# Running batch 1's whole first FFT stage ahead of the FFN, with wide loads and early weights

## The chip, the core and the metric

One core of a Trainium2 chip. The metric is device time in microseconds (us) of one execution. Each profile is that of one of the timed runs; its span is some 2 us shorter than the run's time, because the time also holds what lies outside the first and last instruction. Some names recur: `dZ`, `dU` are the DRAM copies of two intermediates, `zt`, `ut` the SBUF tiles that they are read back into, and a *slot* is one step of the FFN loop: one group of matmuls with W_in (`psH`, then ReLU and square) and one with W_out (`psO`), 1.74 us of TensorE at full clock.

## The reference, cut

```python
def _attn_ref(x, filt_r, filt_i):                 # x: (8, 3008, 256)
    X = np.fft.rfft(x, axis=1)
    Y = X * (filt_r + 1j * filt_i)[None, :, :]    # one global filter, 1505 x 256
    return np.fft.irfft(Y, n=x.shape[1], axis=1).astype(np.float32)

def _moe_ref(x, w_in, w_out):                     # x: (24064, 256); W: 256 x 2048, 2048 x 256
    h = np.maximum(x @ w_in, 0.0)
    return (h * h @ w_out).astype(np.float32)
```

The second follows on the first: an FFT along the sequence, a product with the filter F, the inverse FFT, then an FFN with a squared ReLU.

## The kernel before

The FFT is done by matmuls in stages. Stage A (`psA`, result u) is followed by a change of layout, stage B (`psB`), the product with F on VectorE (`prod`), stage P (`psP`, result ze), a trip through DRAM (`dZ`, `zt`) and stage Y (`psY`, result yt). yt feeds the FFN. Batch 0 runs first, with nothing beside it; from then on each next batch's stages are put between the FFN's matmuls, slot by slot. Batch 0 has its own stage A: x is the stationary operand, and ScalarE and VectorE evict each PSUM bank into a transposed copy, uT.

```python
def chunk_a0(c):                               # batch 0, c = 0..3
    for k in range(2):
        for dt in range(2):
            ...                                # 8 matmuls of 96 columns into ps
            m = 32 * c + 16 * k
            o = uT[:, dt, :, m:m + 16].rearrange("p c (m q) -> p m c q", q=4)
            pv = ps[:, 0:384].rearrange("p (m c q) -> p m c q", m=4, q=4)
            if dt == 0: nc.scalar.copy(out=o, in_=pv)
            else:       nc.vector.tensor_copy(out=o, in_=pv)
```

uT is `[128, 2, 24, 128]` in float16, so for a fixed c the index m, q runs over neighbours and c steps by 128 elements, 256 bytes. PSUM is read in order, and each run of four q is 8 bytes side by side in SBUF.

What surrounds the FFN's start, in program order (`...` marks cuts):

```python
for r in range(14):                            # batch 0: stages B and P
    ...
    if r in (5, 8):
        load_x(1, r // 8); cast_x(1, r // 8, nc.gpsimd)    # 96-row tiles
    if r == 10: read_z(0, 0, (0,))
read_z(0, 1, (0,))
for c in range(2): read_z(0, c, (1,))
for c in range(2): chunk_a(1, c)               # half of batch 1's stage A
load_wout(); load_x(1, 2); load_x(1, 3)
for c in range(2, 4): read_z(0, c)
for c in range(2): write_u(1, c)
keep_warm(10)
for n in range(4): unit_y(0, n)                # then the FFN starts
...
for p in range(12):                            # batch 1's products, in slots 16 to 33
    r = t0 + (17 if b == 1 else 19) * p // 11
    put(r, 0, unit_b, b, p); put(r, 0, unit_s, b, p); put(r + 2, 1, unit_p, b, p)
```

Pools that matter: two x32 buffers, three u buffers, three ze buffers. A ze or u buffer is free again only when the DMA that wrote it to DRAM has landed (experiments 5 and 8 show such waits: 6.35 us for a u buffer, 5.26 us for a ze buffer).

## Time and profile before

| | us |
|---|---|
| median of the first three runs | 823.59 (821.54 to 827.16) |
| profiled run, its span | 826.93, 824.8 |
| ScalarE's table load (ACT_TABLE_LOAD): starts, takes | 12.02, 1.28 |
| last eviction of batch 0's stage A starts | 24.6 |
| first dZ write issued | 41.58 |
| output group of slot 8, slot 34, slot 40 starts | 75.84, 142.37, 156.69 |

The views that the prediction rests on stand in it. The first is the tile view of uT in the kernel before: line, engine, operation, count, then least, median and greatest ns of one instruction, the times of the first and last start, and the shapes.

```profile
L377 ACT CAST uT<-psA x8: 478/478/479, 14.0 to 24.2; 128x384 f16<-128x384 f32 x8
L379 DVE CAST uT<-psA x8: 557/557/558, 15.5 to 24.6; 128x384 f16<-128x384 f32 x8
```

```profile
20.00:40.00 20.00, 17.19 (x213) 14.94 (x211) 13.47 (x15) 12.14 (x17) 4.85 (x5) 0.97 0.52 192
```

The reader is to see that an eviction of 384 elements takes about half a microsecond (0.48 us on ScalarE, 0.56 on VectorE), and that TensorE is at almost full clock here (0.97).

### The profile page before, as it was taken

To read this page: it belongs to the slowest core of one execution; us is meant where nothing else is said; L and a number is where in the kernel's file an instruction comes from. 1 tells how busy PE (TensorE), PEld (TensorE's weight loads), DVE (VectorE), ACT (ScalarE), POOL (GpSimd) and SP (SyncE) were. 2 spreads that over 40 slices of the span, in tenths; PEclk is the share of its full clock that TensorE was granted. 3 is DMA by queue.
4 is the path that set the end of the run, shared out by engine and by line. 5 is a ranking of instruction groups with operands and counts; after the bars stand their busy time and mean duration, and the time that the engine had idled before them with its cause. 6 is when DMAs were issued, how large, how long until landed. Compare 5 with 4: busy or idle time off the path is not lost.

```text
span 824.8 us, 14748 instructions
## 1 busy us (share of the span) xinstructions
PE 787.3 (95%) x6080; PEld 553.7 (67%) x6080; DVE 547.7 (66%) x874; ACT 553.4 (67%) x708; POOL 32.6 (4%) x45
## 2 busy tenths in 40 slices
PE   5878987999999999999999999999999999999998
PEld 3744654666767667776668666786767767676666
DVE  4656566557975599656995579755995569654432
ACT  1655764676777777677777767776777767766664
POOL 4210132000000000000000000000000000000000
PEclk7998999999999999999999999999999999999999
DMA  9488454533681554624563346715555242431111
GB/s 367 174 243 205 141 141 118 126 93 126 165 205 41 142 163 128 170 63 156 141 174 83 105 144 166 187 37 169 133 145 143 64 153 77 108 73 39 39 39 52
DMA packets 87930, 107.94 MB, mean 131 GB/s; under 512 B 6208, under 2 KB 78656, under 8 KB 83392
## 3 DMA queue, kind: packets, MB, share of 16 engines
q1 hardware_dynamic: 87512, 106.59, 46.0%
q8 instruction: 47, 0.77, 0.4%
q10 hardware_dynamic: 288, 0.43, 0.2%
q14 instruction: 19, 0.16, 0.1%
q0 software_dynamic: 64, 0.00, 0.0%
HBM read 58.76 MB, written 48.23 MB: 130 GB/s over the span
## 4 chain that ended last, share of the span: by engine, by line
PE 83%; DMA 8%; DVE 6%; POOL 2%; ACT 1%; issue 1%; SPq 0%; POOLq 0%; DVEq 0%; ACTq 0%
PE psO L530 36%; PE psH L515 34%; PE psA L327 3%; PE psY L485 2%; DMA ut<-dU 2%; PE psB L408 2%; DVE prod L411 2%; PE psP L444 2%; DMA wout<-in_moe_w_out_dram 1%; DVE h L523 1%; DMA x<-in_x_dram 1%; DMA dZ<-ze 1%; DMA zt<-dZ 1%; POOL yf L420 1%; POOL yf L419 1%
## 5 line engine op out<-in xcount | busy, mean ns | idle before, releaser
L519 ACT ACTIVATE h<-psH 128x1024 f16<-128x1024 f32 x376 | 384.9, 1024 | 199.9 <-PE psH L515 197.5
L530 PE MATMUL psO<-sWout,h 128*128 128x256 f16 x3008 | 390.7, 273 | 3.3 <-DVE h L523 3.3
L515 PE MATMUL psH<-yt,sWin 128*128 128x512 f16 (+7 forms) x1728 | 389.0, 353 | 3.1 <-DVE yt L494 2.5
L530 PEld LDWEIGHTS <-h 128*128 128x128 f16 x3008 | 291.3, 98 | 83.6 <-DVE h L523 3.9
L523 DVE TENSOR_TENSOR h<-h 128x1024 f16<-128x1024 f16 x376 | 254.0, 685 | 101.3 <-ACT h L519 99.9
L515 PEld LDWEIGHTS <-sWin 128*128 128x128 f16 x1728 | 159.9, 98 | 104.1 <-issue 6.2
L411 DVE TENSOR_TENSOR prod<-psB,sF 128x1024 f16<-128x1024 f32 x96 | 116.7, 1220 | 9.7 <-PE psB L408 6.5
L494 DVE CAST yt<-psY 128x376 f16<-128x376 f32 x64 | 35.1, 549 | 62.2 <-PE psY L485 62.2
L446 ACT CAST ze<-psP 128x512 f16<-128x512 f32 x96 | 55.9, 585 | 28.6 <-PE psP L444 25.1
L334 DVE CAST u<-psA 96x512 f16<-96x512 f32 x52 | 35.7, 687 | 49.5 <-PE psA L327 49.5
L537 ACT COPY ost<-psO 128x512 f32<-128x512 f32 x94 | 55.5, 590 | 7.5 <-PE psO L530 5.8
L426 DVE TENSOR_TENSOR yf<-prod,yf 128x512 f16<-128x512 f16 x84 | 35.7, 425 | 19.4 <-POOL yf L420 16.9
L485 PEld LDWEIGHTS <-zt 112*128 112x128 f16 x512 | 34.8, 98 | 15.8 <-issue 6.2
L485 PE MATMUL psY<-sC,zt 112*128 112x94 f16 x512 | 42.1, 205 | 2.8 <-DMA zt<-dZ 1.4
L327 PE MATMUL psA<-x,sC 94*96 94x512 f16 x104 | 40.1, 386 | 0.9 <-DVE x L313 0.9
L408 PE MATMUL psB<-ut,sSB 128*128 128x256 f16 x192 | 36.6, 272 | 3.3 <-DVE prod L411 2.3
L444 PE MATMUL psP<-yf,sSP 128*128 128x256 f16 x168 | 32.1, 273 | 4.1 <-DVE prod L411 3.0
L408 PEld LDWEIGHTS <-sSB 128*128 128x128 f16 x192 | 18.6, 98 | 24.7 <-issue 6.0
L492 ACT CAST yt<-psY 128x376 f16<-128x376 f32 x64 | 29.8, 467 | 4.1 <-PE psY L485 4.0
L313 DVE CAST x<-x 94x2048 f16<-94x2048 f32 x26 | 31.6, 1216 | 0.0
L332 ACT CAST u<-psA 96x512 f16<-96x512 f32 x52 | 29.8, 572 | 0.4 <-PE psA L327 0.4
L419 DVE COPY yf<-prod 64x512 f16<-64x512 f16 x72 | 20.9, 290 | 2.5
(53 smaller groups left out, 229.7 us busy)
## 6 DMA issues: line engine op xcount, KB each, us to landing
x<-in_x_dram SPq DMA_DIRECT2D x24, 768.0 KB
dZ<-ze SPq DMA_DIRECT2D x32, 384.0 KB
zt<-dZ SPq DMA_DIRECT2D x64, 192.0 KB
dU<-u SPq DMA_DIRECT2D x28, 384.0 KB
out_dram<-ost SPq DMA_DIRECT2D x32, 256.0 KB
out_dram<-ost SPq DMA_DIRECT2D x64, 128.0 KB
ut<-dU SPq DMA_DIRECT2D x7, 1024.0 KB
ut<-dU SPq DMA_DIRECT2D x7, 512.0 KB
```

The source lines that it names most:

```text
L327: nc.tensor.matmul(ps[0:96, :], sSA, x16s[(b, c)][:, 2 * i:2 * i + 2, :], start=True, stop=True)
L334: nc.vector.tensor_copy(out=o, in_=pv)
L408: nc.tensor.matmul(ps[:, i * D:(i + 1) * D], sSB[:, 2 * p + i, :], uts[b][:, 2 * p + i, :], start=True, stop=True)
L411: nc.vector.tensor_mul(out=prod, in0=ps.rearrange("p (a d) -> p a d", d=D).unsqueeze(1).to_broadcast([128, 2, 2, D]), in1=sF[:, :, 2 * p:2 ...
L444: nc.tensor.matmul(ps[:, i * D:(i + 1) * D], sSP[:, c2, :], prod[:, i, :], start=True, stop=True)
L446: nc.scalar.copy(out=zes[(b, c)][:, 2 * i6:2 * i6 + 2, :], in_=ps.rearrange("p (a d) -> p a d", d=D))
L485: nc.tensor.matmul(ps[:, 94 * jj:94 * jj + 94], zt[:, 4 * (g % 2) + jj, dt * 128:(dt + 1) * 128], sSY, start=True, stop=True)
L515: nc.tensor.matmul(ps[:, i, o:o + n], sWin[:, dt, jt * 128:(jt + 1) * 128], yts[b][:, dt, r:r + n], start=(dt == 0), stop=(dt == 1))
L519: nc.scalar.activation(out=h2[:, 2 * s:2 * s + 2, :], in_=ps, func=AF.Relu)
L523: nc.vector.tensor_mul(out=v, in0=v, in1=v)
L530: nc.tensor.matmul(pso[g][:, t % 2, :], h2s[g][:, jt, t * 128:(t + 1) * 128], sWout[:, jt, :], start=(jt == 0), stop=(jt == NJT - 1))
L537: nc.scalar.copy(out=ost, in_=pso[g])
```

## The change

The intent: have everything that batch 1 and the FFN need ready before the FFN starts, so that the slots hold fewer waits. Batch 1's stage A runs whole ahead of the FFN, on the same wide tiles (128 rows) that batch 0 uses; to share the weights `s0`, their columns are put in the order (q, c). W_in loads early into the x buffers, W_out in two halves, the first ahead of the last dZ write. The u read moves from slot 12 to 4, and batch 1's twelve products spread over slots 8 to 33. F is cast behind stage A, and a tiny ScalarE copy pulls its table load to the start (it starts at 1.61 us in the changed kernel, at 12.02 before).

```diff
-    S0 = S0.reshape(128, 6, 2, 2, NC).transpose(0, 1, 4, 2, 3)
...
+    nc.scalar.copy(out=zero[0:1, 0:1], in_=zero[0:1, 1:2])     # table load early
     keep_warm(14)
... in chunk_a, batch 1
-                nc.tensor.matmul(banks[i][0:96], sSA, x16s[(b, c)][:, m, :], start=True, stop=True)
+                nc.tensor.matmul(o, s0[:, c // 2, :], xw16[(b, 2 * (c % 2))][:, m, :],
+                                 start=True, stop=False)
+                nc.tensor.matmul(o, s0[0:120, 2 + c, :], xw16[(b, 1)][0:120, m, :],
+                                 start=False, stop=True)
... in chunk_a0, batch 0
-                o = uT[:, dt, :, m:m + 16].rearrange("p c (m q) -> p m c q", q=4)
-                pv = ps[:, 0:384].rearrange("p (m c q) -> p m c q", m=4, q=4)
+                o = uT[:, dt, :, m:m + 16].rearrange("p c (m q) -> p m q c", q=4)
+                pv = ps[:, 0:384].rearrange("p (m q c) -> p m q c", m=4, q=4)
... in the plan of slots, b == 1
-        put(12 if b == 1 else 14, 1, read_u, b)
-        t0 = 16 if b == 1 else 18
+        put(4 if b == 1 else 14, 1, read_u, b)
+        t0 = 8 if b == 1 else 18
-            r = t0 + (17 if b == 1 else 19) * p // 11
+            r = t0 + (25 if b == 1 else 19) * p // 11
... ahead of the FFN
-        if r in (5, 8):
-            load_x(1, r // 8)
-            cast_x(1, r // 8, nc.gpsimd)
+        for k in {5: (0,), 8: (1, 2)}.get(r, ()):
+            load_wide(1, k)
+            cast_wide(1, k, nc.gpsimd)
         if r == 10:
             read_z(0, 0, (0,))
+            load_wout(0)
+    for k in range(2):
+        cast_wout(k, nc.gpsimd)
     read_z(0, 1, (0,))
+    chunk_a(1, 0)
+    chunk_a(1, 2)
     for c in range(2):
         read_z(0, c, (1,))
-    ...                                                        # as printed above
+    write_u(1, 0); chunk_a(1, 1); write_u(1, 2); load_wout(1)
+    for n in range(2): unit_y(0, n)
+    chunk_a(1, 3)
+    for n in range(2, 4): unit_y(0, n)
+    write_u(1, 1); write_u(1, 3)
```

With the new column order, the eviction of batch 0 reads PSUM in order again, but the innermost index is now c: it writes single elements, 256 bytes apart.

More of the change, by code (lines that the diff above doesn't have):

```diff
@@ L210, with load_wide, cast_wide @@
     nc.scalar.dma_start(out=sPF, in_=dPF.ap().rearrange("p (w q) -> p w q", q=128))
-    x0 = []
-    v0 = xrows[0:2048, :].rearrange("(p m) d -> p m d", m=16)
-    v1 = xrows[2048:3072, :].rearrange("(p m) d -> p m d", m=8)
-    for k, v in enumerate((v0[:, 0:8, :], v1, v0[:, 8:16, :])):
-        t = (p_h2 if k == 2 else p_x32).tile([128, 8, D], F32, tag="h2" if k == 2 else "x32",
-                                             name=f"x0_{k}")
-        nc.sync.dma_start(out=t, in_=v)
-        x0.append(t)
+    xw32, xw16 = {}, {}
+    def load_wide(b, k):
+        v0 = xrows[b * S:b * S + 2048, :].rearrange("(p m) d -> p m d", m=16)
+        v1 = xrows[b * S + 2048:b * S + 3072, :].rearrange("(p m) d -> p m d", m=8)
+        pool = p_h2 if (b, k) == (0, 2) else p_x32
+        t = pool.tile([128, 8, D], F32, tag="h2" if pool is p_h2 else "x32", name=f"xw_{b}_{k}")
+        nc.sync.dma_start(out=t, in_=(v0[:, 0:8, :], v1, v0[:, 8:16, :])[k])
+        xw32[(b, k)] = t
+    def cast_wide(b, k, eng):
+        t = p_x16.tile([128, 8, D], F16, tag="x16", name=f"xw16_{b}_{k}")
+        for i in range(2):
+            m = slice(4 * i, 4 * i + 4)
+            eng.tensor_copy(out=t[:, m, :], in_=xw32[(b, k)][:, m, :])
+        xw16[(b, k)] = t
+    for k in range(3):
+        load_wide(0, k)
     f32s = []
@@ L289, with load_win, cast_win, load_wout @@
     w32s = {}
-    def load_win():
-        w32s[0] = p_h2.tile([128, 2, DFF], F32, tag="h2", name="win32")
-        nc.sync.dma_start(out=w32s[0], in_=moe_w_in.rearrange("(t r) j -> r t j", r=128))
-    def load_wout():
-        w32s[1] = p_h2.tile([128, NJT, 256], F32, tag="h2", name="wout32")
-        nc.sync.dma_start(out=w32s[1], in_=moe_w_out.rearrange("(jt r) c -> r jt c", r=128))
-    def cast_win():
-        for k in range(4):
-            nc.gpsimd.tensor_copy(out=sWin[:, :, 512 * k:512 * k + 512],
-                                  in_=w32s[0][:, :, 512 * k:512 * k + 512])
-    def cast_wout(k):
-        nc.vector.tensor_copy(out=sWout[:, 4 * k:4 * k + 4, :],
-                              in_=w32s[1][:, 4 * k:4 * k + 4, :])
+    def load_win(k):
+        w32s[k] = p_x32.tile([128, DFF], F32, tag="x32", name=f"win32_{k}")
+        nc.sync.dma_start(out=w32s[k], in_=moe_w_in[128 * k:128 * k + 128, :])
+    def cast_win(k):
+        for j in range(2):
+            c = slice(1024 * j, 1024 * j + 1024)
+            nc.gpsimd.tensor_copy(out=sWin[:, k, c], in_=w32s[k][:, c])
+    def load_wout(k):
+        if k == 0:
+            w32s[2] = p_h2.tile([128, NJT, 256], F32, tag="h2", name="wout32")
+        c = slice(8 * k, 8 * k + 8)
+        nc.sync.dma_start(out=w32s[2][:, c, :],
+                          in_=moe_w_out.rearrange("(jt r) c -> r jt c", r=128)[:, c, :])
+    def cast_wout(k, eng=nc.vector):
+        c = slice(4 * k, 4 * k + 4)
+        eng.tensor_copy(out=sWout[:, c, :], in_=w32s[2][:, c, :])
     x16s, us, uts, prods, zes, zts, yts = {}, {}, {}, {}, {}, {}, {}
@@ L345, in chunk_a @@
                 m = slice(4 * k + 2 * i, 4 * k + 2 * i + 2)
-                nc.tensor.matmul(banks[i][0:96], sSA, x16s[(b, c)][:, m, :],
-                                 start=True, stop=True)
+                o = banks[i][0:96]
+                nc.tensor.matmul(o, s0[:, c // 2, :], xw16[(b, 2 * (c % 2))][:, m, :],
+                                 start=True, stop=False)
+                nc.tensor.matmul(o, s0[0:120, 2 + c, :], xw16[(b, 1)][0:120, m, :],
+                                 start=False, stop=True)
             eng = pair_engine()
@@ L368, in chunk_a0 @@
                     d = slice(128 * dt, 128 * dt + 128)
-                    nc.tensor.matmul(o, x016[2 * (c % 2)][:, m, d], s0[:, c // 2, :],
+                    nc.tensor.matmul(o, xw16[(0, 2 * (c % 2))][:, m, d], s0[:, c // 2, :],
                                      start=True, stop=False)
-                    nc.tensor.matmul(o, x016[1][0:120, m, d], s0[0:120, 2 + c, :],
+                    nc.tensor.matmul(o, xw16[(0, 1)][0:120, m, d], s0[0:120, 2 + c, :],
                                      start=False, stop=True)
                 m = 32 * c + 16 * k
-                o = uT[:, dt, :, m:m + 16].rearrange("p c (m q) -> p m c q", q=4)
-                pv = ps[:, 0:384].rearrange("p (m c q) -> p m c q", m=4, q=4)
+                o = uT[:, dt, :, m:m + 16].rearrange("p c (m q) -> p m q c", q=4)
+                pv = ps[:, 0:384].rearrange("p (m q c) -> p m q c", m=4, q=4)
                 if dt == 0:
@@ L567, in fft_plan @@
                     unit_y, 0, n)
-            for k in range(4):
-                put(3 + k, 1, cast_wout, k)
-            for c in range(2, 4):
-                put(3 + 2 * c, 0, cast_x, 1, c)
-        t0 = 4 if b == 1 else 6
-        for a in range(8 if b == 1 else 0, 16):
+            for k in range(2, 4):
+                put(2 + k, 1, cast_wout, k)
+        t0 = 6
+        for a in range(0 if b > 1 else 16, 16):
             put(t0 + a // 2, a % 2, unit_a, b, a)
-        put(12 if b == 1 else 14, 1, read_u, b)
-        t0 = 16 if b == 1 else 18
+        put(4 if b == 1 else 14, 1, read_u, b)
+        t0 = 8 if b == 1 else 18
         for p in range(12):
-            r = t0 + (17 if b == 1 else 19) * p // 11
+            r = t0 + (25 if b == 1 else 19) * p // 11
             put(r, 0, unit_b, b, p)
@@ L602, in run @@
             f(*a)
-    x016 = [p_x16.tile([128, 8, D], F16, tag="x16", name=f"x016_{k}") for k in range(3)]
     uT = p_h2.tile([128, 2, NC, 128], F16, tag="h2", name="uT")
     for k, eng in enumerate((nc.vector, nc.vector, nc.gpsimd)):
-        for i in range(2):
-            m = slice(4 * i, 4 * i + 4)
-            eng.tensor_copy(out=x016[k][:, m, :], in_=x0[k][:, m, :])
-    f16s.append(p_h2.tile([128, 2, QF + D], F16, tag="h2", name="f16"))
-    for im in range(2):
-        nc.gpsimd.tensor_copy(out=f16s[0][:, im, QF:], in_=nyq[:, im, :])
-        for e in (slice(0, 1504), slice(1504, QF)):
-            nc.gpsimd.tensor_copy(out=f16s[0][:, im, e], in_=f32s[im][:, e])
+        cast_wide(0, k, eng)
     def load_const(t, d, k):
@@ L626 @@
         load_const(sSPx[k], dSPx, k)
+    for k in range(2):
+        load_win(k)
     for c in (0, 2, 1, 3):
         chunk_a0(c)
+    f16s.append(p_h2.tile([128, 2, QF + D], F16, tag="h2", name="f16"))
+    for im in range(2):
+        nc.gpsimd.tensor_copy(out=f16s[0][:, im, QF:], in_=nyq[:, im, :])
+        for e in (slice(0, 1504), slice(1504, QF)):
+            nc.gpsimd.tensor_copy(out=f16s[0][:, im, e], in_=f32s[im][:, e])
+    for k in range(2):
+        cast_win(k)
     uts[0] = p_ut.tile([128, NC, D], F16, tag="ut", name="ut_0")
@@ L631 @@
         turn_u(k)
-    load_win()
-    cast_win()
     for k, eng in enumerate((nc.vector, nc.scalar, nc.vector)):
@@ L645 @@
             unit_p(0, r - 2)
-        if r in (5, 8):
-            load_x(1, r // 8)
-            cast_x(1, r // 8, nc.gpsimd)
+        for k in {5: (0,), 8: (1, 2)}.get(r, ()):
+            load_wide(1, k)
+            cast_wide(1, k, nc.gpsimd)
         if r == 10:
             read_z(0, 0, (0,))
+            load_wout(0)
+    for k in range(2):
+        cast_wout(k, nc.gpsimd)
     read_z(0, 1, (0,))
+    chunk_a(1, 0)
+    chunk_a(1, 2)
     for c in range(2):
         read_z(0, c, (1,))
-    for c in range(2):
-        chunk_a(1, c)
-    load_wout()
-    load_x(1, 2)
-    load_x(1, 3)
+    write_u(1, 0)
+    chunk_a(1, 1)
+    write_u(1, 2)
+    load_wout(1)
+    for n in range(2):
+        unit_y(0, n)
+    chunk_a(1, 3)
+    for n in range(2, 4):
+        unit_y(0, n)
+    prologue[0] = False
+    write_u(1, 1)
+    write_u(1, 3)
     for c in range(2, 4):
         read_z(0, c)
-    for c in range(2):
-        write_u(1, c)
-    keep_warm(10)
-    for n in range(4):
-        unit_y(0, n)
-    prologue[0] = False
     work = {}
```

## The prediction

> **What bounds the kernel now.** I read the page's busy table and slices first, then busy time by stretch, then the chain of waits, then each engine's timeline from 40 to 165 us.
>
> ```profile
> PE 787.3 (95%) x6080; PEld 553.7 (67%) x6080; DVE 547.7 (66%) x874; ACT 553.4 (67%) x708; POOL 32.6 (4%) x45
> PE   5878987999999999999999999999999999999998
> ```
>
> From slice 9 on (165 us) TensorE is never idle, so the change, which ends its work near 160 us, can only save gaps before that. By stretch (PE, PEld, DVE, ACT, POOL busy, granted clock, DMA share, GB/s):
>
> ```profile
> 40.00:60.00 20.00, 16.02 (x115) 10.49 (x113) 12.12 (x13) 11.86 (x18) 4.96 (x4) 0.91 0.82 218
> 60.00:80.00 20.00, 15.13 (x77) 7.16 (x75) 12.40 (x20) 10.90 (x15) 0.00 (x0) 0.83 0.94 243
> 100.00:120.00 20.00, 16.69 (x124) 11.21 (x122) 13.07 (x19) 12.32 (x17) 6.03 (x11) 1.00 0.46 126
> 120.00:140.00 20.00, 14.94 (x106) 9.56 (x103) 13.40 (x19) 10.62 (x14) 5.70 (x10) 1.00 0.34 92
> 160.00:180.00 20.00, 20.00 (x179) 14.05 (x178) 11.58 (x20) 14.18 (x21) 0.00 (x0) 1.00 0.23 61
> ```
>
> Two holes: 40 to 80 us, where the DMA engines are full and the clock falls, and 100 to 140, where DMA is half idle. The chain names the first:
>
> ```profile
> 56.11 12.32 DMA wout<-in_moe_w_out_dram
> 74.28 1.14 DVE x L313
> 76.05 1.71 PE psO L530 x8
> ```
>
> W_out is asked for at 56.1 us and lands at 68.4, VectorE casts it until 73.7 and then casts an x tile. The first FFN output group (eight psO matmuls, slot 8) starts at 75.84 and takes 1.71 us where others take 0.87, because the clock is at half from 72.5 to 79.3. The timelines name the second hole (VectorE row, then TensorE row):
>
> ```profile
> 128.67 0.43 DVE L426 TENSOR_TENSOR yf<-prod,yf 128x512 f16<-128x512 f16 x1 [1.43 <-POOL yf L420]
> 132.03 0.39 PE L444 MATMUL psP<-yf,sSP 128*128 128x256 f16 x2 [2.66 <-DVE prod L411]
> ```
>
> For batch 1 the half swap runs on GpSimd (two copies of 0.61 us) and the add that needs it stands next on VectorE's queue: every one of the 12 products costs VectorE about 1.2 + 1.4 of waiting + 0.35 = 2.95 us. TensorE then waits for it.
>
> I count in slots, the kernel's FFN step: g1 (4 matmuls of 512, 0.87 us), g2 (8 of 256, 0.87), so 1.74 us for TensorE. The output group of slot 8 starts at 75.84, of slot 16 at 94.45, of slot 34 at 142.37, of slot 40 at 156.69. From slot 40 on the two programs do the same.
>
> [...] half clock from 55.4 to 58.8, 72.5 to 79.3 and 140.7 to 144.1 us, each after a gap. [...] the 96-row x loads move 233 GB/s with the engines full (68 to 70 us), the 128-row loads of batch 0 move 420 to 434 (4 to 12 us). [...] the packets of the x loads issued just behind W_out begin only as W_out's end (64 us). So a transfer issued early delays those issued after it.
>
> **The change part by part.**
>
> *Start.* A tiny ACT copy pulls the table load to about 2 us. Before, the first eviction of stage A waited until 14.03 (table load, then a GpSimd cast that this instruction waits for; the new order has no such wait). The second x tile is cast by 10.75, so it can now run at about 10.8: 3.2 us earlier. The last two chunks need the GpSimd cast at 14.0 anyway and TensorE is at half clock, so I take 2.5 us for the end of stage A (24.6 to 22.1). The evictions now scatter single 2-byte elements; I assume their 0.48 and 0.56 us stay. The F casts are bound by the landing of F (15.6 and 19.2 us), done at 22, not on the path. Everything up to the last product of batch 0 moves by 2.5 us: the four dZ writes, issued before at 41.58, 45.12, 48.97 and 52.08, are ready at 39.1, 42.6, 46.5 and 49.6.
>
> *DMA before the FFN.* W_in moves to the idle stretch behind the constants (DMA is at 0.16 from 24 us, 0.00 from 26): no gain by itself, its cast at 41 us was early enough. But three 1 MB x loads (2.5 us each: 128 packets of 309 ns over 16 engines) and half of W_out (1024 packets of 51 ns, 3.3 us) now stand in the same ring with the dZ writes (1.5 us each) ahead of the z reads that the FFN waits for. The third x load also waits for the GpSimd cast of the first (same buffer). In ring order from 39.8: dZ 1.7, x 2.6, dZ 1.5, x 2.6, x 2.6, dZ 1.5, z read 0.5, half W_out 3.3, dZ 1.5: 17.8 us, so the last dZ lands at about 58.3 instead of 55.2. The z read behind it took 3.3 us before (landed 58.6): it lands at 61 to 61.5, 2.5 us later than now.
>
> *FFN start.* Between the first z transforms stands chunk 3 of batch 1: 8 matmuls of 512. TensorE has idled since about 55, so it is at half clock: 8 x 0.43 = 3.4 us. Four z transforms of about 0.5 us and an eviction of 0.5: g1 of slot 0 runs freely from about 67, against 61.8 now: 5 us lost.
>
> *Slots 0 to 8.* W_out is ready by then (first half cast on GpSimd, second landing at about 67, cast in slots 4 and 5). What is left is ScalarE: 8 ReLUs at about 1.0 us, 2 z evictions at 0.4 and one g1: 9.5 us. Slot 8's output group starts at 76.5 to 77, against 75.84: the 14.0 us of now (61.8 to 75.84) become 9.5 to 10, and the later start eats it.
>
> *Slots 8 to 34.* Now 66.5 us (75.84 to 142.37). TensorE's need after: 26 x 1.74 = 45.2, 24 pairs of B and P matmuls x 0.22 = 5.2, 8 z transforms x 0.16 = 1.3: 51.7 us. VectorE's need from the first product (slot 8) to the twelfth (slot 33): 11 x 2.95 = 32.5, 25 squares x 0.60 = 15, 4 z evictions x 0.46 = 1.8, 2 x casts x 1.14 = 2.3: 51.6 us for 25 slots in which TensorE needs 49.4. So they are nearly even. The same sum checks the old kernel: slots 16 to 34 hold 12 products (35.4), 18 squares (10.8), 2 casts (2.3) and 2 evictions (0.9) = 49.4, and took 47.9. With the slack of about two slots between a square or sum and its reader I give 2 us of stall: about 53.7. Saved: 12.8. Of it 2.5 is the half clock at 75 to 79, 1.7 the eight stage A matmuls that left, the rest the VectorE queue.
>
> *Slots 34 to 40.* Now 14.3. The half clock (3.4 us, 1.7 lost) followed a 2.06 us gap that should go; the wait for the z read in slot 39 (1.1 us) stays. 12.6: saved 1.7.
>
> *Sum.* Slot 40 at 76.7 + 53.7 + 12.6 = 143.0 against 156.69: 13.7 us. 823.6 - 13.7 = 809.9, say 810 us, 1.65% less.
>
> **The rivals.** First: the ring does not bind before the FFN, and the program gains what its plan intends, a start at about 58 us. For it: x loads of 128 rows are quick, and DMA is idle from 36 to 42 us. Against: the x loads stand behind the first dZ on the same queue, so that idle time is not used. It would give 16 to 20 us in all, about 805. Second: VectorE becomes the bound of slots 8 to 34 for good, since its 51.6 us hold no slack for products that come late and for the order in the queue. Then that part takes 57 to 58 us and the time is about 814. Third: the FFN start slips more, because W_out's half and dU writes hold up batch 1's u read, which TensorE needs as early as slot 8. My ring order has it land at about 74 for a need at 76; 3 us more would show fully: 813 to 815. A loss against the kernel before would need all of these together.
>
> **Range and chances.** The largest terms are the FFN start (61.8 to 67, uncertain by 3) and the stall in slots 8 to 34 (by 2.5); together about 4 to 5 us either way. So 803 to 817. Faster by over 2% means under 807.1: 0.25. Within 2%: 0.73. Slower: 0.02.
>
> **What would show it.** Right: the last z read ahead of slot 0 lands at 60 to 62 and the first g1 matmuls run at half clock or just after it; no wait for W_out; slot 8 near 76.5; slot 40 near 143; TensorE's waits on VectorE small between 80 and 130; the same pace afterwards. Wrong: an FFN start before 60 or after 70, a wait on the u read at slot 8, waits for VectorE over 5 us in slots 8 to 34, or any change of pace after slot 40.

## The result, and the profile after

The changed kernel is correct and takes 833.65 us (median of four, 830.75 to 834.18), against 822.57 us (820.89 to 827.16, four runs). The ratio is 1.0119, with a 95% interval of 1.007 to 1.0167. Here and below, a ratio is the mean time of one kernel's runs over that of the other's of the same rounds, so not quite the ratio of the medians. The change made the kernel about 1.2% slower, within the 2% that counts as the same; 810 us was predicted.

One caution for what follows. The profiled run of before (826.93 us) was one of its slower ones, and that of the changed kernel (830.75) its fastest. Step by step the profiles can only account for the 3.8 us between those two runs, not for the 9.8 us that the ratio makes of 823 us.

The tile view of uT in the changed kernel, in the columns explained above:

```profile
L395 ACT CAST uT<-psA x8: 1864/1868/2218, 10.8 to 29.2; 128x384 f16<-128x384 f32 x8
L397 DVE CAST uT<-psA x8: 1865/1978/2097, 13.6 to 30.4; 128x384 f16<-128x384 f32 x8
```

The same number of elements and the same types, but 1.87 and 1.98 us (medians) instead of 0.48 and 0.56. ScalarE's timeline shows it one by one (start, duration, engine, line, operation, and in brackets the idle time before and what ended it):

```profile
10.80 1.86 ACT L395 CAST uT<-psA 128x384 f16<-128x384 f32 x1 [7.70 <-PE psA L389]
14.19 1.87 ACT L395 CAST uT<-psA 128x384 f16<-128x384 f32 x1 [1.53 <-PE psA L389]
```

The first starts at 10.80 us, where before it was 14.03. So the head start of 3.2 us is there, but each of these evictions takes 1.4 us more, and the head start is lost within the stage. It ends with an eviction that starts at 30.4 us, not 24.6.

The busy slices of TensorE and its granted clock on the page of the changed kernel, then its stretches:

```profile
PE   5686989999999999999999999999999999999998
PEclk7597999999999999999999999999999999999999
```

```profile
20.00:40.00 20.00, 12.29 (x122) 11.11 (x120) 13.93 (x11) 11.41 (x9) 6.19 (x6) 0.54 0.48 193
60.00:80.00 20.00, 12.70 (x51) 6.67 (x52) 4.53 (x8) 5.53 (x9) 6.76 (x7) 0.74 0.89 247
100.00:120.00 20.00, 18.75 (x144) 12.84 (x142) 12.47 (x19) 13.30 (x19) 4.89 (x8) 1.00 0.20 59
120.00:140.00 20.00, 18.77 (x143) 13.06 (x140) 13.34 (x20) 13.38 (x17) 4.89 (x8) 1.00 0.54 146
```

Between 20 and 40 us TensorE runs at little over half clock (0.54 against 0.97): it is busy for 12.29 us of 20, and over all of batch 0's stage A its matmuls wait 8.7 us in four gaps for the evictions. The hole from 100 to 140 us has gone as intended: 18.75 and 18.77 us of TensorE instead of 16.69 and 14.94. But the stretch ahead of the FFN, 60 to 80, is emptier than before.

How the first z read gets there is in the DMA queue's issues, the chain of waits and TensorE's timeline of the changed kernel:

```profile
50.88 0.38 SPq L467 DMA_DIRECT2D dZ<-ze  x1
```

```profile
62.79 9.69 DMA dZ<-ze
72.54 3.30 DMA zt<-dZ
```

```profile
75.88 0.50 PE L503 MATMUL psY<-sC,zt 112*128 112x94 f16 x4 [4.17 <-DMA zt<-dZ]
```

The first dZ write is issued at 50.88 (41.58 before, 39.1 predicted); the last takes 9.69 us from issue to landing; TensorE waits 4.17 us for the z read. The steps side by side, with the run that mends the evictions (next section) added:

| us | before | predicted | changed | evictions mended |
|---|---|---|---|---|
| first dZ write issued | 41.58 | 39.1 | 50.88 | 37.32 |
| first z transform starts (predicted: z read lands) | – | 61.3 | 75.88 | 63.98 |
| g1 runs freely | 61.8 | 67 | 81.90 | 70.87 |
| slot 8 | 75.84 | 76.7 | 91.84 | 80.81 |
| slot 34 | 142.37 | 130.4 | 147.77 | 136.7 |
| slot 40 | 156.69 | 143.0 | 161.2 | 149.9 |
| span | 824.8 | – | 829.0 | 819.0 |

From slot 40 to the end all twelve profiles take 667 to 669 us. So what there is to explain lies ahead of slot 40.

### The profile page after: what moved, and what is told of

The parts are those of the page before.

```text
span 829.0 us, 14766 instructions
## 1 busy us (share of the span) xinstructions
PE 790.5 (95%) x6086; PEld 559.4 (67%) x6086; DVE 553.9 (67%) x869; ACT 564.8 (68%) x708; POOL 37.1 (4%) x51
## 4 chain that ended last, share of the span: by engine, by line
PE 83%; DMA 6%; DVE 6%; ACT 2%; POOL 1%; issue 1%; SPq 0%; DVEq 0%; POOLq 0%; ACTq 0%
PE psO L548 36%; PE psH L533 35%; PE psA L342 3%; PE psY L503 2%; PE psB L426 2%; DMA ut<-dU 2%; PE psP L462 2%; DVE prod L429 2%; DVE h L541 2%; DMA dZ<-ze 2%; ACT uT L395 1%; DMA xw<-in_x_dram 1%; DMA zt<-dZ 1%; POOL yf L438 1%; POOL yf L437 1%; DVE uT L397 1%
## 5 line engine op out<-in xcount | busy, mean ns | idle before, releaser
L349 DVE CAST u<-psA 96x512 f16<-96x512 f32 x48 | 33.0, 687 | 45.1 <-PE psA L342 45.1
L503 PEld LDWEIGHTS <-zt 112*128 112x128 f16 x512 | 35.2, 98 | 18.2 <-DMA zt<-dZ 4.8
L342 PE MATMUL psA<-x,sC 94*96 94x512 f16 x96 | 36.6, 382 | 0.0
L328 DVE CAST x<-x 94x2048 f16<-94x2048 f32 x24 | 29.2, 1217 | 0.0
L347 ACT CAST u<-psA 96x512 f16<-96x512 f32 x48 | 27.5, 572 | 0.0
L395 ACT CAST uT<-psA 128x384 f16<-128x384 f32 x8 | 14.5, 1996 | 13.8 <-PE psA L389 13.8
```

The source lines that it names most:

```text
L342: nc.tensor.matmul(ps[0:96, :], sSA, x16s[(b, c)][:, 2 * i:2 * i + 2, :], start=True, stop=True)
L503: nc.tensor.matmul(ps[:, 94 * jj:94 * jj + 94], zt[:, 4 * (g % 2) + jj, dt * 128:(dt + 1) * 128], sSY, start=True, stop=True)
```

## The experiments

Each kernel is an edit of the changed kernel unless it says otherwise; each gave correct results. Where a ratio stands, it is against the runs of before on the same chip.

### 1. The evictions mended

Theory: the single-element writes cost 1.4 us each and delay everything by about 12 us. Rival: the loss lies in the new DMA order. The new column order is kept; only the order in which the eviction walks is turned, so that PSUM is read with a step and uT written in runs of four.

```diff
-   o = uT[...].rearrange("p c (m q) -> p m q c", q=4)
-   pv = ps[:, 0:384].rearrange("p (m q c) -> p m q c", m=4, q=4)
+   o = uT[...].rearrange("p c (m q) -> p m c q", q=4)
+   pv = ps[:, 0:384].rearrange("p (m q c) -> p m c q", m=4, q=4)
```

> The changed kernel, with one thing altered: the sixteen stage A evictions of batch 0 walk PSUM with a stride and write the same addresses in runs of four 2-byte elements (8 bytes), as the kernel before did, instead of single elements 256 bytes apart. Theory W (single 2-byte writes are what costs): the evictions fall from 1.87 and 1.98 us to about 0.5 and 0.6 us, the first dZ write is issued near 39 to 40 us instead of 50.9, and the time falls by 10 to 13 us to 821 to 824, about the kernel before. Rival R (any step that is not one element costs, on the reading side as well): the evictions stay above 1 us and the time stays above 828. Rival D (the ring of DMA transfers sets the FFN start anyway): the evictions get short, but the time falls by less than 5 us.

Measured: 820.72 us (820.17 to 820.86); before 824.58; ratio 0.9954 (0.993 to 0.9978). Its tile view of uT and its stretch from 20 to 40 us:

```profile
L395 ACT CAST uT<-psA x8: 479/479/480, 10.9 to 20.0; 128x384 f16<-128x384 f32 x8
L397 DVE CAST uT<-psA x8: 557/558/558, 12.0 to 20.4; 128x384 f16<-128x384 f32 x8
```

```profile
20.00:40.00 20.00, 18.14 (x194) 15.57 (x191) 14.75 (x15) 14.93 (x19) 6.25 (x6) 1.00 0.59 219
```

The old durations are back, the stage's last eviction starts at 20.4, and the clock is 1.00. By the two ratios, 1.0119 against 0.9954, the write order alone cost some 13 us; rivals R and D both fall. It also shows that the rest of the change gains about 4 us, not 13.7: the evictions are the largest part of the miss, not all of it. The last eviction starts 10.0 us sooner than in the changed kernel (20.4 against 30.4), the first dZ write 13.6 us sooner (37.32 against 50.88): the rest is lost behind the evictions, where the changed kernel's TensorE stays at half clock until about 38.3 us.

### 2. The same writes put into the kernel before

```diff
  (the kernel before)
-   S0 = S0.reshape(128, 6, 2, 2, NC).transpose(0, 1, 4, 2, 3)
-   o = uT[...].rearrange("p c (m q) -> p m c q", q=4)
-   pv = ps[:, 0:384].rearrange("p (m c q) -> p m c q", m=4, q=4)
+   o = uT[...].rearrange("p c (m q) -> p m q c", q=4)
+   pv = ps[:, 0:384].rearrange("p (m q c) -> p m q c", m=4, q=4)
```

> The kernel before, with nothing changed but the column order of the stage A constant and with it the single-element writes of the changed kernel. Theory W: evictions of 1.9 to 2.0 us, stage A ends 11 to 13 us later than now (near 37 us), and since everything up to the FFN hangs on it the time rises by the same, to 833 to 837. If the time rises by under 5 us, the evictions are not what sets the start of the FFN, and the loss of the changed kernel has another cause.

Measured: 838.12 us (833.41 to 839.87), ratio 1.0158 (1.012 to 1.0195). The stretch of this kernel from 20 to 40 us:

```profile
20.00:40.00 20.00, 12.64 (x144) 11.98 (x143) 14.94 (x10) 13.03 (x10) 2.15 (x2) 0.59 0.23 89
```

The evictions take 1.87 and 1.98 us here too (medians of 8), and TensorE falls to a clock of 0.59 with nothing else changed. Adding the writes to one kernel costs 1.6% (838 us, a little above the expected 833 to 837), and taking them out of the other gains as much. That settles their size. The first eviction starts at 14.12 us, so the earlier start in the changed kernel does not come from the column order. Whether the early table load or the GpSimd cast that no longer stands in front brought it, no run tells apart. By the trace of the kernel before, the cast ended last (the table load was over at 13.30, the eviction started at 14.03), so the early table load alone would hardly have done it.

### 3. What exactly is slow: four run lengths in one kernel

The four chunks, in the order in which they run (0, 2, 1, 3), write runs of 1, 2, 8 and 16 elements.

```diff
+   if c == 0:   ...  "p c (m q) -> p m q c", q=4       # single elements
+   elif c == 2: ...  "p c (m q) -> p m c q", q=2       # pairs
+   elif c == 1: ...  "p c (m q) -> p m c q", q=8
+   else:        pv = pv.rearrange("p (q c) -> p c q", q=16)
```

> The changed kernel, with a different run length of the eviction's writes in each of the four chunks of stage A, in the order in which they run: single elements, runs of 2 (4 bytes), of 8 (16 bytes), of 16 (32 bytes). If the cost is one write per run of up to some bytes, the 384 elements take about 1.87 us, 1.0 us, 0.5 us and 0.5 us (ScalarE), a halving from 1 to 2 and no further gain past 4. [...] If reading PSUM with a stride costs too, none comes down to 0.48 us.

Measured in one look, of unknown state: 822.58 us. ScalarE's second eviction of single elements, then its first of pairs, of eights and of sixteens:

```profile
13.76 1.87 ACT L405 CAST uT<-psA 128x384 f16<-128x384 f32 x1 [1.14 <-PE psA L389]
17.15 0.50 ACT L405 CAST uT<-psA 128x384 f16<-128x384 f32 x1 [1.53 <-PE psA L389]
19.71 0.48 ACT L405 CAST uT<-psA 128x384 f16<-128x384 f32 x1 [0.79 <-PE psA L389]
22.60 0.48 ACT L405 CAST uT<-psA 128x384 f16<-128x384 f32 x1 [0.96 <-PE psA L389]
```

Neither outcome named beforehand came true: the pairs take 0.50 us and not 1.0, and with PSUM read with a step the eights and sixteens still come down to 0.48 us. The cost does not fall little by little with the run's length. It is there for single elements and gone for pairs of 4 bytes (0.50 us, against 0.48 for runs of 8 and 16). A single element costs 1.39 us / 384 = 3.6 ns more on ScalarE. The strided reading of PSUM (a step of 96 bytes) costs next to nothing on either engine, as run 1 already showed: 479 and 558 ns there, against 478 and 557 in order.

Why single elements are slow this does not show: no run varies the distance of 256 bytes.

### 4. The x loads taken out of the ring ahead of the FFN

The evictions stay slow here. The three wide x loads of batch 1 move from rounds 5 and 8 to a place behind W_in, where the DMA engines of the changed kernel are idle (busy share 0.03 from 30 to 32 us, 0.00 from 32 to 40).

```diff
+   load_wide(1, 0); load_wide(1, 1); cast_wide(1, 0, nc.gpsimd); load_wide(1, 2)
+   for k in (1, 2): cast_wide(1, k, nc.gpsimd)          # ahead of the rounds
    ...
-        for k in {5: (0,), 8: (1, 2)}.get(r, ()):
-            load_wide(1, k)
-            cast_wide(1, k, nc.gpsimd)
```

> The changed kernel with its single-element evictions kept, but with the three x loads of batch 1 and their casts moved to straight behind the W_in casts, into the idle stretch of the DMA engines ahead of the first dZ write. Theory Q (the x loads stand in the ring between the dZ writes and the z reads, and delay them): the z read that slot 0 waits for lands near 69 us instead of 75.9, the first free g1 matmul moves from 81.9 to about 74 or 75, and the time falls by 6 to 8 us to 826 to 828. If the ring is not what delays the z reads, nothing moves by more than 2 us.

Measured: 826.56 us (825.97 to 827.07), ratio 1.0026 (1.0005 to 1.0047), 7.1 us under the changed kernel by the medians, 0.9% by the ratios, as expected in time. The chain of waits in this kernel:

```profile
61.61 6.43 DMA dZ<-ze
68.12 3.50 DMA zt<-dZ
```

The last dZ write takes 6.43 us to land instead of 9.69, and the first z transform starts at 71.67: 20.6 us after the first dZ write (51.11), not 25.0. That is half of what was expected: g1 runs freely from 78.15 instead of 81.90, not from 74 or 75. The DMA ring ahead of the FFN is thus a true bound, apart from the evictions. By the two profiled runs the gain is 3.7 us only (spans 825.3 and 829.0), which is the caution from above: the changed kernel's profile is its fastest run. Where the rest of the 7.1 us lies the profiles do not show.

### 5. The first half of W_out behind the z reads

From here on each kernel has the mended evictions, and is compared with run 1.

```diff
         if r == 10:
             read_z(0, 0, (0,))
-            load_wout(0)
-    for k in range(2):
-        cast_wout(k, nc.gpsimd)
     ...
     for c in range(2):
         read_z(0, c, (1,))
+    load_wout(0)
+    for k in range(2):
+        cast_wout(k, nc.gpsimd)
     write_u(1, 0)
```

> The changed kernel with writes in runs of four (the first experiment), and the first half of W_out issued behind the z reads of the first two chunks instead of ahead of the last dZ write. There the z read that slot 0 waits for landed at 63.9 us and TensorE stood 6.5 us. Theory Q (everything that is issued ahead of the last dZ write delays the z read by its own packets): half a W_out is 1024 packets of about 51 ns over 16 engines, 3.3 us; the z read lands at 60 to 61, and the time falls by 2.5 to 3.5 us from 820.7 to about 817 to 818. Rival (the z read waits for the dZ writes' own slow completion or for a late engine): less than 1 us.

Measured: 823.08 us (821.17 to 824.64), ratio 1.001 (0.9979 to 1.0042). A miss: nothing gained on run 1's 0.9954, rather lost. The wait for the z read in run 1, then that in this kernel with its next long wait, then ScalarE in this kernel:

```profile
63.98 0.49 PE L503 MATMUL psY<-sC,zt 112*128 112x94 f16 x4 [6.47 <-DMA zt<-dZ]
```

```profile
62.20 0.50 PE L503 MATMUL psY<-sC,zt 112*128 112x94 f16 x4 [3.05 <-DMA zt<-dZ]
70.66 0.37 PE L501 MATMUL psY<-zero 128*128 128x256 f16 x1 [4.67 <-ACT u L372]
```

```profile
69.60 1.01 ACT L372 CAST u<-psA 96x1024 f16<-96x1024 f32 x1 [6.35 <-DMA dU<-u]
```

The z read did come sooner: 23.7 us after the first dZ write (38.55) instead of 26.7. (In this profile the first dZ write itself came 1.2 us later than in run 1, with the same program up to there.) But W_out's half now stood in the ring ahead of the u write of chunk 0, and chunk 3 needs that buffer, one of three. Its eviction waited 6.35 us for the write to land, and the z transforms behind it waited along. The theory about the ring was right in kind (62.2 instead of the expected 60 to 61), and the gain went into a new wait that I had not looked for.

### 6. W_out behind the u writes too

If that reading is right, W_out behind both the z reads and the u writes of chunks 0 and 2 must keep the gain.

```diff
  (against run 1; the early load_wout(0) and its casts removed)
     write_u(1, 2)
+    load_wout(0)
     load_wout(1)
+    for k in range(2):
+        cast_wout(k, nc.gpsimd)
```

> The kernel with evictions in runs of four, and the first half of W_out issued behind the u writes of chunks 0 and 2, so that neither the z reads nor those u writes stand behind it. In the run that put it just behind the z reads of chunks 0 and 1, the z read came 3.0 us sooner after the first dZ write (23.7 instead of 26.7 us), but then chunk 3's eviction waited 6.4 us for the u write of chunk 0 (one of three u buffers), and all was given back. Theory 1 (the FFN start is bound by what stands ahead in the DMA ring, first z reads, then u writes): z read again 23 to 24 us after the first dZ write, no wait of chunk 3's evictions for the u write over 2 us, slot 8's output group 39.5 to 41 us after the first dZ write instead of 43.5, 817 to 818.5 us. Theory 2 (what is taken away here always comes back at the next transfer: W_out itself, or the u read, becomes the wait at slot 8): slot 8 43 us or more after the first dZ write with a wait for W_out's cast or the u read, 820 to 823 us.

Measured: 817.94 us (815.97 to 818.09), ratio 0.9913 (0.9871 to 0.9954). ScalarE's wait for the u write, and the first wait of slot 8 on TensorE:

```profile
63.56 1.01 ACT L372 CAST u<-psA 96x1024 f16<-96x1024 f32 x1 [1.01 <-DMA dU<-u]
```

```profile
78.45 0.38 PE L426 MATMUL psB<-ut,sSB 128*128 128x256 f16 x2 [0.83 <-DMA ut<-dU]
```

The first theory holds nearly as written: the z read comes 24.6 us after the first dZ write (61.66 and 37.10; 23 to 24 expected), the wait for the u write is 1.01 us, slot 8 comes 41.6 us after the first dZ write (39.5 to 41 expected, 43.5 in run 1). A little of the second shows as well: the u read is now the last to arrive at slot 8, by 0.83 us. Over run 1 (0.9954, 0.993 to 0.9978) the gain in time is not clear of noise, as the two intervals overlap; over run 5 it is.

### 7. All loads early, and the sums one slot later

Three kernels on run 1. The first moves both halves of W_out and the x loads ahead of the first dZ write:

```diff
+    load_wout(0); load_wide(1, 0); load_wide(1, 1); cast_wide(1, 0, nc.gpsimd)
+    load_wide(1, 2)
+    for k in (1, 2): cast_wide(1, k, nc.gpsimd)
+    load_wout(1)
+    for k in range(4): cast_wout(k, nc.gpsimd)           # and their old places removed
```

> The changed kernel with writes in runs of four, and both W_out halves and all three x loads of batch 1 (with their casts on GpSimd) issued into the idle stretch of the DMA engines behind W_in, ahead of the first dZ write. Nothing then stands between the dZ writes and the z reads. Theory Q: the z read lands at 55 to 57 us, the first free g1 matmul runs at 58 to 61 instead of 70.9, and the time falls by 9 to 12 us from 820.7, to 809 to 812: what the change was meant to give. If it stays above 816, something else than the ring holds the start of the FFN.

Measured: 812.15 us (811.37 to 813.75), ratio 0.9881 (0.9853 to 0.9908), just above what was expected. Slot 8 comes at 73.39 instead of 80.81; g1 runs freely from 63.73, later than the expected 58 to 61.

The second changes one word of the plan for slots 8 to 34. VectorE's sum waits there for GpSimd's swap of the product just made; one slot later, the swap is nearly done.

```diff
-            put(r, 0, unit_s, b, p)
+            put(r + (b == 1), 0, unit_s, b, p)
```

> The changed kernel with writes in runs of four, and for batch 1 the add of the two product halves put one slot later, so that VectorE no longer stands for GpSimd's two copies in its queue. Theory V (VectorE with its 1.4 us of waiting per product is what makes slots 8 to 34 last 55.9 us, where TensorE needs 51.7): the waits go, slots 8 to 34 last 52 to 53.5 us, and the time falls by 2.5 to 4 us to 817 to 818. If ScalarE or TensorE's own order is the bound there, less than 1 us changes.

Measured: 817.45 us (817.15 to 819.21), ratio 0.9947 (0.992 to 0.9974). The median is 3.3 us under run 1's, but by the ratios (0.9954) the difference is not shown. By the profile, slots 8 to 34 take 53.6 us instead of 55.9. The waits for the swap fall from 16.9 us in twelve to 11.9; they do not go, as was expected. That stretch is what the edit can reach, so I read its gain as 2.3 us.

The third has both edits.

> Both of the above: all loads early, writes in runs of four, and batch 1's add one slot later. If the two gains are of different stretches they add up: 806 to 809 us, below both kernels. If the earlier FFN start makes new waits (the u read at slot 8, or VectorE), it ends near the all-early kernel's time or above.

Measured: 811.47 us (809.89 to 813.62), ratio 0.9864 (0.9832 to 0.9895). That is 0.7 us under the first of the three, a difference that the ratios do not show, and misses what was expected: the gains did not add up. The stretches of the two profiles say why not. Slots 8 to 34 took 53.8 us here and 56.1 without the late sums, so the 2.3 us are there; but slot 8 came at 74.92 instead of 73.39. The first freely running g1 matmuls without the late sums, then with them:

```profile
63.73 1.67 PE L533 MATMUL psH<-yt,sWin 128*128 128x512 f16 x7 [0.49 <-DVE yt L512]
```

```profile
64.04 5.08 PE L533 MATMUL psH<-yt,sWin 128*128 128x512 f16 x15 [0.49 <-DVE yt L512]
```

Seven in 1.67 us is full clock. Of the fifteen in 5.08 us, which take 3.92 with their gap in the first kernel, a part runs at half clock. The stretches around them, without the late sums, then with them:

```profile
61.00:64.50 3.50, 2.18 (x17) 1.10 (x16) 1.77 (x2) 1.00 (x2) 0.00 (x0) 1.00 0.66 169
64.50:68.00 3.50, 3.17 (x18) 1.39 (x16) 1.56 (x3) 3.17 (x4) 0.00 (x0) 1.00 1.05 250
```

```profile
61.00:64.50 3.50, 1.67 (x15) 0.90 (x14) 1.77 (x2) 1.32 (x2) 0.00 (x0) 1.00 0.64 162
64.50:68.00 3.50, 3.50 (x10) 1.28 (x9) 0.92 (x2) 2.05 (x2) 0.00 (x0) 0.51 1.05 248
```

In both profiles TensorE had come to full clock by 56 us. With the late sums it falls back to half from 64.6 to 68.0 us, without them it does not. The two programs are the same up to slot 8 on TensorE, so this lies in the two executions and not in the edit. From 56 us to the fall TensorE's gaps were of at most 0.78 us here, and it was busy for 1.67 of the last 3.5 us before it; the half clock lasted 3.4 us. In the kernel before it came at 140.7 us, after a gap of 2.06 us, and lasted 3.4 us too. What sets it off is not shown. Which of the two is the more frequent these profiles do not show.

### 8. The second half of W_out back in its place

With all loads early the first dZ write was issued at 39.8 us, but the last only at 52.1, where run 1 has 37.3 and 47.9. ScalarE of the kernel with all loads early, at the eviction into ze:

```profile
49.79 1.07 ACT L464 CAST ze<-psP 128x512 f16<-128x512 f32 x2 [5.26 <-DMA dZ<-ze]
```

All three ze buffers were waiting to be written out, behind the second half of W_out. (In the third kernel of 7, which is edited here, this wait is 4.49 us.) So that half goes back behind the z reads and u writes, the rest stays as in the third kernel of 7.

```diff
-    load_wout(1)
-    for k in range(4):
+    for k in range(2):
         cast_wout(k, nc.gpsimd)
     ...
     write_u(1, 2)
+    load_wout(1)
  (and its two casts again in slots 4 and 5)
```

> The kernel with all loads early and the sums put one slot later (811.5 us), but with the second half of W_out back at its old place, behind the z reads of chunks 0 and 1. In that kernel the fourth dZ write was issued only at 51.8 us although the first was issued at 40.1, because ScalarE waited about 5 us for a ze buffer whose dZ write had to land first, and W_out's second half stood just ahead of those writes. Theory 1 (that half was in the way): the wait of ScalarE for a dZ write falls under 2.5 us, the last dZ write is issued near 48, slot 8's output group starts near 71.5 instead of 74.9, 807 to 809.5 us. Theory 2 (the x loads alone hold the first dZ write, and the late half only moves the wait to the u writes or to slot 8): slot 8 stays within 1 us of 74 to 75, 810.5 to 813 us.

Measured: 809.75 us (807.27 to 810.32), before 822.77, ratio 0.9809 (0.9759 to 0.9859). ScalarE's wait in the third kernel of 7, then in this one, then the first wait of slot 8 on TensorE here:

```profile
49.51 1.07 ACT L464 CAST ze<-psP 128x512 f16<-128x512 f32 x2 [4.49 <-DMA dZ<-ze]
```

```profile
47.18 1.07 ACT L464 CAST ze<-psP 128x512 f16<-128x512 f32 x2 [3.85 <-DMA dZ<-ze]
```

```profile
72.00 0.38 PE L426 MATMUL psB<-ut,sSB 128*128 128x256 f16 x2 [1.03 <-DMA ut<-dU]
```

Slot 8 comes at 72.22 (71.5 expected, 74.9 before the edit), the last dZ write is issued at 49.4. But little of that is shown to be the edit. ScalarE was 1.7 us ahead before the edit can act (an eviction into ze that starts at 37.05 us in the third kernel of 7, ahead of W_out's second half at 39.56, starts at 35.35 here), and that kernel's profile lost some 1.2 us to the half clock. What depends less on the start is how long the first dZ write takes to land; from the chain of waits, in the third kernel of 7 and here:

```profile
40.08 9.32 DMA dZ<-ze
```

```profile
39.18 7.90 DMA dZ<-ze
```

That is 1.4 us less, where the prediction put half of W_out at 3.3. The wait of ScalarE fell from 4.49 to 3.85 us and not under 2.5. The x loads still stand ahead, and they hold up the queue too: the first dZ write is issued at 39.18, as soon as the three x loads, which take 8.20 us of SyncE's queue, are out. Of the first theory the direction holds, not its sizes; and the u read now comes last at slot 8, as the second had it. This kernel has the lowest median of all versions tried, 1.9% (1.4 to 2.4) less than the kernel before; that it is faster than the third kernel of 7 is not shown, as the intervals of the two ratios overlap.

## Why the prediction was wrong

**The step that failed** is the sentence "The evictions now scatter single 2-byte elements; I assume their 0.48 and 0.56 us stay." They took 1.87 and 1.98 us. The change to the writes was seen, and its cost was set to zero by assumption, with no row behind it: no instruction of the profile before wrote single elements. Sixteen slow evictions, eight on each engine and alternating with matmuls at half clock, put the first dZ write at 50.88 instead of 39.1: 11.8 of the 18.2 us by which slot 40 missed its prediction (161.2 against 143.0). Runs 1 and 2 show the size from both sides, and run 3 that single elements are the reason.

**The start** was otherwise right. The first eviction was predicted at 10.8 us and came at 10.80. With mended evictions, the first dZ write is issued at 37.32, 1.8 us sooner than predicted; TensorE's granted clock there is 0.91 from 0 to 20 us and 1.00 from 20 to 40, against 0.78 and 0.97 in the kernel before, where the prediction reckoned with half clock.

**The DMA before the FFN** had the right mechanism and the wrong size. From the first dZ write to the z read 22.2 us were predicted; the changed kernel took 25.0 to the first transform and run 1 took 26.7. Taking out x loads (run 4) gives back 4.4 us of it, and taking out W_out's half (run 5) 3.0, about the 3.3 that the prediction put down for that half. The ring sum was thus right in kind and 2.8 to 4.5 us too small. (Its terms, 39.8 and 17.8, make 57.6 and not the 58.3 that is written, so the terms alone are short by 0.7 more.) It assumed that the ring is never empty; in the changed kernel the third x load kept the queue waiting, 2.1 us of it for a GpSimd cast (the two x issues took 6.12 us of the queue), and in run 1 the DMA engines were busy for 0.88 of the time from 40 to 60 us. How much of the excess that is, and how much slower transfers, was not separated.

**The FFN start and slots 0 to 8** held. From the first transform to free g1 5.7 us were predicted, 6.0 and 6.9 (run 1) measured; from there to slot 8 9.5 to 10, and 9.94 measured in both. No wait for W_out showed.

**Slots 8 to 34** took 55.9 us, with 53.7 predicted and 66.5 before. The part that gains was right. The stall was taken as 2 us and was 4.2: the sum that follows its product directly on VectorE's queue. Placing it one slot later takes 2.3 of it away and gives 53.6. The prediction's second rival, VectorE as the bound of this part (57 to 58 us), was thus half true.

**Slots 34 to 40** took 13.45 against 12.6. The prediction took the whole loss of the half clock (140.7 to 144.1 us, 1.7 lost) off this stretch, but slot 34 starts at 142.37, so only half of it lay inside: 14.32 less 0.87 is 13.45, just what was measured. The terms sum up: 11.8 + 2.8 + 0.3 + 0.2 + 2.2 + 0.85 = 18.2 us. The pace after slot 40 did not change, as predicted.

**The rivals.** The first, a ring that does not bind, fell with the 25.0 us and run 4. The third, a u read that is late at slot 8, never cost much: at slot 8 the changed kernel does not wait for it at all, and runs 6 and 8 wait 0.83 and 1.03 us. The sentence that a loss "would need all of these together" was the weakest: each rival varied the waits, and none varied the duration of an instruction whose form had changed. The range of 803 to 817 was too narrow for the same reason. That the outcome lies within 2%, to which 0.73 was given, is luck: the prediction got there by way of a gain of 13.7 us, and the runs show a loss.

**Left open:** the 6 us by which the ratio (9.8 us) and the two profiled runs (3.8 us) differ, which no profile places; the F casts behind stage A, which no run took alone; why single elements are slow, since no run varies their distance; what sends the clock to half; and why the 96-row x loads moved 233 GB/s where the 128-row loads moved 420 to 434, since no run varies the rows alone.

## What to carry to other kernels

An instruction that keeps its shape but changes the order of its elements is a new instruction: take its time from a row with the same innermost step or count it as unknown, and if an order must change, do as here: let the PSUM reading step and keep SBUF writes in runs of at least two 16-bit elements (0.50 us here for pairs, 1.87 for single elements). A transfer taken from the head of a ring pays only if you also follow the next buffers that ring sets free (in run 5 the next one brought a wait of 6.35 us). Before a gain is claimed from two profiles, look where those two runs lie among the timed ones, and count from an event that the edit cannot have moved.
